# Tracing the first batch's attention without its order behind the latest exponential and maximum

## The chip, the cores and the metric

The kernel runs on one core of a Trainium2 chip. The metric is the device time of one execution in microseconds (us); of the kernel before there are three runs, and their median counts.

Five engines work side by side, each through its own queue of instructions: TensorE (PE, matmuls, with weight loads PEld), VectorE (DVE), ScalarE (ACT), GpSimd (POOL) and SyncE (SP, which here issues nearly all DMAs). Data lies in SBUF; matmuls write to PSUM, which has eight banks per core.

## The reference: what is computed

Attention with a threshold, then a token-mixing block with a channel MLP, then a gated MLP with a convolution over tokens. Cut to what matters (4 batches, 8 heads, 576 tokens, head size 64):

```python
scores = scale * np.matmul(q, k.transpose(0, 1, 3, 2))
thresh = np.max(scores, axis=-1, keepdims=True) - tau
scores = np.where(scores >= thresh, scores, -1e9)
attn = np.exp(scores - np.max(scores, axis=-1, keepdims=True))
attn = attn / (np.sum(attn, axis=-1, keepdims=True) + 1e-09)
x = np.matmul(attn, v)                       # heads side by side: [4, 576, 512]
h = np.maximum(x^T @ w_tok1, 0) @ w_tok2     # token mixing, 576 -> 256 -> 576
u = x + h^T
h2 = np.maximum(u @ w_ch1, 0) @ w_ch2        # channels, 512 -> 1536 -> 512
y = u + h2
g = np.maximum(y @ w_in, 0)                  # 512 -> 1024
out = (g * sigmoid(conv3(g, conv_w))) @ w_out
```

## The kernel before, in words

**Precision and weights.** Most matmuls run on pairs of 16-bit tiles, a high part and the rest; the scores of the first two batches are float32. The weights come as 64-bit numbers and are turned into such pairs once, in pieces of up to 512 columns. Each piece is loaded by SP into one of three stage buffers (`st`, L118), unpacked on ACT (L155, L156), DVE (L157, L159) and sometimes POOL (L153, L143), then split (ACT L144, POOL L145). A stage buffer is free for the next load when L159 has read it.

**Attention.** A batch has four pairs of heads. A pair is worked in nine *slots* of 128 rows of queries (slot 4 of a pair holds 64 rows of either head), so a batch has 36 slots, numbered here through the batch from 0. A slot goes through these steps:

- scores (PE, L308): four matmuls of 128x288 into a pair of PSUM banks; three such pairs take turns in the first batch, so slot i+3 needs mask i to be done
- maximum (DVE, L324, tile `nm`), limit (ACT, L334, `thr`), exponential (ACT, L336), mask (DVE, L343: exponential times "score at least the limit")
- half (ACT, L348: the 16-bit high part), rest (POOL, L352), then a transposing DMA from SP (L357), "transpose i" below
- the product with V (PE, L367 and L370), five slots later

In the first batch the exponential, the halves and the transposed tile of a slot lie in `act_t`, in four sets that take turns: exponential i+4 waits for rest i, half i+4 for transpose i to land, transpose i+4 for product i. After slots 4 and 8 of a pair the products are normalised (DVE L383, L384, L387, L390) and split (ACT L395, POOL L396) into `x`. When both are there, the pair's token mixing follows (`tok`: PE L407 and L422, L427, ACT L412, L429, DVE L413, L430) and gives that pair's part of `u`. The next pair's Q, K and V are loaded by SP (L236, L240, L268) into the tiles of the pair before the last, scaled (ACT L244, POOL L272) and split (ACT L273, POOL L274).

**Dense stages.** `dense(b)` runs the channel MLP and the gated MLP of batch b on PE (L547, L565, L598, L621), and the attention of batch b+1 is traced between its steps. The first of them, L547, needs all four parts of `u`.

**What sets the order.** The program is traced step by step and then put in order by a list scheduler, which gives each engine, in time of its own estimate, the earliest traced instruction whose inputs are ready. The order is fixed when the kernel is built; on the chip an engine takes its instructions in that order. `attention(b)` is a generator with four steps per slot i: exponential work of slot i; mask and half of slot i-1; product of slot i-5, rest and transpose of slot i-1 and scores of slots up to i+2; then the work of `prep` and `tok`. `exps` stores its maximum and its exponential in `crit`. `steps` (L438) wraps the generator and traces each step inside `tc.issue_after` of these two: every ACT instruction of the step gets an edge that keeps it behind the latest exponential traced so far, every DVE instruction one that keeps it behind the latest maximum. These are orders within one queue and cost no semaphore. Only the first batch's attention is wrapped so; the weight steps are traced outside of it.

Of the kernel before, what the change touches and what calls it, by code (L numbers as in the profile page):

```python
# [19 lines left out]
def kernel(ctx: ExitStack, tc: tile.TileContext, q, k, v, tau,  # L20
# [8 lines left out]
    B, NPR, _, S = q.shape  # L29
# [150 lines left out]
    def wstep(n):  # L180

        for _ in range(n):
            while wq and len(wrun) < 3:
                wnext()
            if wrun:
                next(wrun.pop(0))
            if wq:
                wnext()
        if n and not wrun and CB not in free:
            free.append(CB)  # L190
# [106 lines left out]
    def where(i):  # L297
        return i // PER, i // NSL % NP, i % NSL
# [22 lines left out]
    def exps(i):  # L321
        c = chk[i]
        nm = sm.tile([P, 1], F32, tag="nm", name="nm")
        crit["max"] = V.tensor_reduce(out=nm, in_=c["s3"], axis=AX.XY, op=ALU.max, negate=True)  # L324
        kind = 0 if i < NB32 * PER else 1
        bias, sc = nm, 1.0
        if kind:
            bias, sc = sm.tile([P, 1], F32, tag="bias", name="bias"), ESC
            A.activation(out=bias, in_=nm, func=AF.Copy, scale=sc)
        thr = sm.tile([P, 1], F32, tag="thr", name="thr")  # L330
        if kind:
            G.tensor_scalar(out=thr, in0=nm, scalar1=-1.0, scalar2=mtaus[:, 1:2], op0=ALU.mult, op1=ALU.add)  # L332
        else:
            A.activation(out=thr, in_=nm, func=AF.Identity, scale=-1.0, bias=mtaus[:, 0:1])  # L334
        e = half(i, 0).bitcast(F32) if i < PER else qk2.tile([P, S], F32, tag="x", name="e", bufs=15)
        crit["exp"] = A.activation(out=e.rearrange("p (a b) -> p a b", a=2), in_=c["s3"], func=AF.Exp, bias=bias,  # L336
                                   scale=sc)
        c.update(thr=thr, e=e)

    def mask(i):  # L340
        c = chk[i]
        e3 = c["e"].rearrange("p (a b) -> p a b", a=2)
        crit["mask"] = V.scalar_tensor_tensor(out=e3, in0=c["s3"], scalar=c["thr"], in1=e3, op0=ALU.is_ge, op1=ALU.mult)  # L343

    def ph(i):
        c = chk[i]
        c["ph"] = half(i, 1) if i < PER else qk2.tile([P, 2 * S], F16, tag="x", name="ph", bufs=15)
        A.activation(out=c["ph"][:, 0:S], in_=c["e"], func=AF.Copy)  # L348

    def rest(i):  # L350
        c = chk[i]
        G.tensor_tensor(out=c["ph"][:, S:], in0=c["e"], in1=c["ph"][:, 0:S], op=ALU.subtract)  # L352
        if i < PER:
            c["pt"] = half(i, 2).rearrange("p (a b) -> p a b", b=P)
        else:
            c["pt"] = qk2.tile([P, NSL, P], F16, tag="x", name="pt", bufs=15)
        turn[i] = nc.sync.dma_start_transpose(out=c["pt"], in_=c["ph"])  # L357
# [80 lines left out]
    def steps(gen, names):  # L438

        while True:  # L440
            with ExitStack() as held:
                for x in names:
                    if x in crit:
                        held.enter_context(tc.issue_after(crit[x].ins))
                try:
                    next(gen)
                except StopIteration:
                    return
            yield

    def attention(b):

        todo, lag = {}, LAGS[b]

        def start(i, gen, gaps):
            for g in gaps:
                todo.setdefault(i, []).append(gen)
                i += g

        c0, c1 = b * PER, (b + 1) * PER  # L460
        for i in range(c0, c1, NSL):
            bb, p, _ = where(i + NSL)
            if bb < B:
                start(i - 1, prep(bb, p), (1, 2, 2, 1, 1, 1))
            start(i + NSL - 1 + lag + 2, tok(b, where(i)[1]), (2, 1, 1))
        if b == 0:
            for _ in prep(0, 0):
                pass
        i = c0 - 1
        while i < c1 + lag or todo:  # L470
            if c0 <= i < c1:
                exps(i)
            yield
            if c0 <= i - 1 < c1:
                mask(i - 1)
                ph(i - 1)
                if i == PER:
                    free.append(5)
            yield
            if c0 <= i - lag < c1:  # L480
                pv(i - lag)
            if c0 <= i - 1 < c1:
                rest(i - 1)
            for j in range(i + 1, i + (3 if i + 2 < PER else 2)):
                if j < c1 and j not in done:
                    scores(j)
                    done.add(j)
            yield
            for g in todo.pop(i, ()):
                next(g, None)  # L490
            yield
            i += 1
# [159 lines left out]
    W0 = [0, 4, 8, 12, 16, 20, 24, 130]  # L652
    HW, HQ = 32, 35
    behind["qk"] = HQ
    for n, _ in enumerate(steps(attention(0), ("exp", "max"))):
        if n == 13:
            behind["w"] = HW
        wstep(W0.count(n))
    na, nq = n + 1, 2 * NF + 6 * NC + 2 * NG + 4 * (NS + 1)
    for b in range(B):  # L660
        att = attention(b + 1) if b + 1 < B else iter(())
        n = 0
# [65 lines left out]
```

## Time and profile before

| | |
|---|---|
| three runs | 793.1, 795.9, 797.14 us; median 795.9 us |
| the profiled execution | 798.93 us; its span 797.1 us |
| PE busy | 742.8 us, 93% of the span |
| DVE busy | 495.5 us, 62% |
| ACT busy | 471.0 us, 59% |
| POOL busy | 421.8 us, 53% |
| DMA, largest queue (from SP) | 55.0% of 16 engines' time |
| granted TensorE clock, mean | 0.981 of full |

How to read it: PE is busy most of the time, but not evenly. The first 126 us hold the first attention and its handover and have most of the low clock; after 300 us PE is almost never idle. Times inside the span are counted from its start. "Idle before" an instruction is the time in which its engine did nothing ahead of it, with the instruction or DMA that ended that wait.

### The profile page before, as it was taken

To read this page: it belongs to the slowest core of one execution; us is meant where nothing else is said; L and a number is where in the kernel's file an instruction comes from. 1 tells how busy PE (TensorE), PEld (TensorE's weight loads), DVE (VectorE), ACT (ScalarE), POOL (GpSimd) and SP (SyncE) were. 2 spreads that over 40 slices of the span, in tenths; PEclk is the share of its full clock that TensorE was granted. 3 is DMA by queue.
4 is the path that set the end of the run, shared out by engine and by line. 5 is a ranking of instruction groups with operands and counts; after the bars stand their busy time and mean duration, and the time that the engine had idled before them with its cause. 6 is when DMAs were issued, how large, how long until landed. Compare 5 with 4: busy or idle time off the path is not lost. (4 is left out here: it accounts for less than half of the span.)

```text
span 797.1 us, 18473 instructions
## 1 busy us (share of the span) xinstructions
PE 742.8 (93%) x7388; PEld 562.1 (71%) x7388; DVE 495.5 (62%) x837; ACT 471.0 (59%) x998; POOL 421.8 (53%) x471
## 2 busy tenths in 40 slices
PE   5579979898998889999999999999999999999998
PEld 3457657676776675678878875788887856887764
DVE  5568877786767683367677892566876960322370
ACT  6768876775766674466566862566565751220371
POOL 5977788877687572155555771265664840000040
PEclk9889989999999999999999999999999999999999
DMA  9989998888789640368676531667664401000001
GB/s 280 195 186 173 166 240 198 187 226 192 200 219 198 106 76 28 93 135 164 135 164 131 117 54 40 139 134 156 143 133 80 76 18 58 1 1 1 2 1 60
DMA packets 195047, 97.84 MB, mean 123 GB/s; under 512 B 174096, under 2 KB 176656, under 8 KB 194960
## 3 DMA queue, kind: packets, MB, share of 16 engines
q1 hardware_dynamic: 194640, 96.39, 55.0%
q8 instruction: 58, 0.95, 0.5%
q10 hardware_dynamic: 320, 0.26, 0.1%
q14 instruction: 29, 0.24, 0.1%
HBM read 42.36 MB, written 4.72 MB: 59 GB/s over the span
## 5 line engine op out<-in xcount | busy, mean ns | idle before, releaser
L352 POOL TENSOR_TENSOR ph<-e,ph 128x576 f16<-128x576 f32 x108 | 141.2, 1308 | 98.0 <-ACT ph L348 93.0
L565 PE MATMUL ps<-act_t,wc_h 128*128 128x256 f16 (+1 forms) x768 | 148.8, 286 | 0.0
L324 DVE TENSOR_REDUCE nm<-ps 128x1 f32<-128x576 f32 x144 | 108.3, 753 | 54.2 <-PE ps L312 27.0
L308 PE MATMUL ps<-kt,qt 128*128 128x288 f32 (+1 forms) x320 | 95.1, 458 | 27.5 <-DVE act_t L343 12.1
L588 POOL TENSOR_TENSOR act_t<-ct,act_t 128x576 f16<-128x576 f32 x32 | 46.6, 1455 | 138.8 <-ACT act_t L587 135.9
L547 PE MATMUL ps<-u_h,wc_h 128*128 128x256 f16 (+1 forms) x384 | 110.0, 287 | 2.0 <-DVE act_t L522 2.0
L547 PE MATMUL ps<-u_h,wc_l 128*128 128x256 f16 (+1 forms) x384 | 109.9, 287 | 0.0
L565 PE MATMUL ps<-act_t,wc_l 128*128 128x256 f16 (+1 forms) x384 | 109.7, 286 | 0.0
L547 PE MATMUL ps<-u_l,wc_h 128*128 128x256 f16 (+1 forms) x384 | 109.4, 287 | 0.0
L343 DVE SCALAR_TENSOR_TENSOR e<-ps,thr,e 128x576 f32<-128x576 f32 x108 | 87.7, 812 | 22.3 <-ACT e L336 9.8
L547 PEld LDWEIGHTS <-wc_h 128*128 128x128 f16 x768 | 75.4, 98 | 20.3 <-issue 1.3
L565 PEld LDWEIGHTS <-wc_h 128*128 128x128 f16 x768 | 75.0, 98 | 18.9 <-issue 0.5
L308 PEld LDWEIGHTS ps<-kt,qt 128*128 128x128 f32 (+1 forms) x320 | 54.1, 197 | 46.2 <-DVE act_t L343 16.5
L367 PE MATMUL ps<-vh,pt 128*128 128x65 f16 (+1 forms) x1080 | 72.1, 195 | 7.4 <-DMA pt<-ph 7.2
L621 PE MATMUL ps<-wo_h,act_t 128*128 128x512 f16 x256 | 76.3, 379 | 1.8 <-DVE u_l L430 1.3
L583 DVE SCALAR_TENSOR_TENSOR ct<-h,cw,ct 128x576 f32<-128x576 f32 x64 | 68.3, 1068 | 15.2 <-ACT ct L581 14.6
L598 PE MATMUL ps<-u_h,wi_h 128*128 128x256 f16 (+1 forms) x256 | 73.0, 286 | 4.3 <-DVE u_l L430 3.2
L367 PEld LDWEIGHTS <-pt 128*128 128x128 f16 (+1 forms) x1080 | 62.7, 101 | 19.3 <-DMA pt<-ph 10.7
L348 ACT ACTIVATE ph<-e 128x576 f16<-128x576 f32 x108 | 73.0, 676 | 2.1 <-DVE e L343 2.1
L598 PE MATMUL ps<-u_h,wi_l 128*128 128x256 f16 (+1 forms) x256 | 73.0, 286 | 0.0
L598 PE MATMUL ps<-u_l,wi_h 128*128 128x256 f16 (+1 forms) x256 | 73.0, 286 | 0.0
L621 PEld LDWEIGHTS <-act_t 128*128 128x128 f16 x384 | 36.7, 98 | 44.0 <-issue 2.1
(113 smaller groups left out, 1621.3 us busy)
## 6 DMA issues: line engine op xcount, KB each, us to landing
st<-in_moe_w_ch_dram SPq DMA_DIRECT2D x24, 512.0 KB, 4.2
ld<-in_v_dram SPq DMA_DIRECT2D x32, 288.0 KB, 3.4
kt<-ks SPq DMA_DIRECT2D x32, 144.0 KB, 2.7
st<-in_moe_w_in_dram SPq DMA_DIRECT2D x8, 512.0 KB, 4.2
st<-in_moe_w_out_dram SPq DMA_DIRECT2D x8, 512.0 KB, 5.2
out_dram<-ot SPq DMA_DIRECT2D x16, 256.0 KB, 2.0
qt<-in_q_dram SPq DMA_DIRECT2D x8, 288.0 KB, 3.9
kt<-in_k_dram SPq DMA_DIRECT2D x16, 144.0 KB, 3.8
```

The costliest lines, as they stand in the source:

```text
L308: T.matmul(s3[o:o + m, a], f32(st["qt"])[:, q0:q0 + m], f32(st["kt"][hh])[:, a * hn:(a + 1) * hn], start=True, stop=True)
L324: crit["max"] = V.tensor_reduce(out=nm, in_=c["s3"], axis=AX.XY, op=ALU.max, negate=True)
L343: crit["mask"] = V.scalar_tensor_tensor(out=e3, in0=c["s3"], scalar=c["thr"], in1=e3, op0=ALU.is_ge, op1=ALU.mult)
L348: A.activation(out=c["ph"][:, 0:S], in_=c["e"], func=AF.Copy)
L352: G.tensor_tensor(out=c["ph"][:, S:], in0=c["e"], in1=c["ph"][:, 0:S], op=ALU.subtract)
L367: T.matmul(dst[o:o + m], pt[:, j, o:o + m], vh[:, hh, j, 0:D + 1], start=(j == 0), stop=(j == NSL - 1))
L547: T.matmul(t, wc1[wx][:, f, c], u[c][ux][:, sl], start=(c == 0 and i == 0), stop=(c == NC - 1 and i == 2))
L565: T.matmul(t, wc2[wx][:, c, f], r_t(f, rx)[:, sl], start=(by_dve(c) and f == 0 and i == 0), stop=(f == NF - 1 and i == 2))
L583: V.scalar_tensor_tensor(out=ct, in0=ht[:, kk:kk + S], scalar=cw[:, kk, f:f + 1], in1=ct, op0=ALU.mult, op1=ALU.add)
L588: G.tensor_tensor(out=g_t(f, 1), in0=ct, in1=g_t(f, 0), op=ALU.subtract)
L598: T.matmul(t, wi[wx][:, f, c], u[c][ux][:, s0:s0 + n], start=(c == 0 and i == 0), stop=(c == NC - 1 and i == 2))
L621: T.matmul(t, g_t(f, gx)[:, j * P:(j + 1) * P], wo[wx][:, f], **lim)
```

## The change

The wrapper around the first batch's attention goes. `steps` and `crit` stay in the file and no longer do anything.

```diff
-    for n, _ in enumerate(steps(attention(0), ("exp", "max"))):
+    for n, _ in enumerate(attention(0)):
```

The scheduler makes another order of the same work, on all engines, up to a place near 285 us of the trace before; behind it the rows of both orders agree on each engine. Most instructions are moved by a few rows. The places that the prediction speaks of:

On DVE, the maxima of slots 10, 11 and 12 (`nm_490`, `nm_515`, `nm_545`), the masks of slots 9, 10 and 11 (`thr_440`, `thr_492`, `thr_517`), the first pair's first normalisation (`rc_473`, `x32_352`) and two weight steps (`st_225`). Before:

```order
L324 TENSOR_REDUCE nm_490<-ps_166 128x1
L324 TENSOR_REDUCE nm_515<-ps_166 128x1
L157 SCALAR_TENSOR_TENSOR ps_166<-st_225,ps_166 128x288
L383 TENSOR_SCALAR rc_473<-ps_166 128x5
L343 SCALAR_TENSOR_TENSOR act_t_165<-ps_166,thr_440,act_t_165 128x576
L384 RECIPROCAL rc_473<-rc_473 128x5
L387 TENSOR_TENSOR x32_352<-ps_166,rc_473 128x4x64
L390 SCALAR_TENSOR_TENSOR x32_352<-ps_166,rc_473,blk_97 128x128
L343 SCALAR_TENSOR_TENSOR act_t_165<-ps_166,thr_492,act_t_165 128x576
L159 SCALAR_TENSOR_TENSOR wf_224<-st_225,ps_166 128x288
L324 TENSOR_REDUCE nm_545<-ps_166 128x1
L343 SCALAR_TENSOR_TENSOR act_t_165<-ps_166,thr_517,act_t_165 128x576
```

And after the change:

```order
L324 TENSOR_REDUCE nm_490<-ps_166 128x1
L343 SCALAR_TENSOR_TENSOR act_t_165<-ps_166,thr_440,act_t_165 128x576
L324 TENSOR_REDUCE nm_515<-ps_166 128x1
L157 SCALAR_TENSOR_TENSOR ps_166<-st_225,ps_166 128x288
L383 TENSOR_SCALAR rc_473<-ps_166 128x5
L384 RECIPROCAL rc_473<-rc_473 128x5
L324 TENSOR_REDUCE nm_545<-ps_166 128x1
L387 TENSOR_TENSOR x32_352<-ps_166,rc_473 128x4x64
L390 SCALAR_TENSOR_TENSOR x32_352<-ps_166,rc_473,blk_97 128x128
L159 SCALAR_TENSOR_TENSOR wf_224<-st_225,ps_166 128x288
L343 SCALAR_TENSOR_TENSOR act_t_165<-ps_166,thr_492,act_t_165 128x576
L343 SCALAR_TENSOR_TENSOR act_t_165<-ps_166,thr_517,act_t_165 128x576
```

Mask 9 has moved ahead of maximum 11 and the normalisation; mask 10 and L159 have moved behind maximum 12.

On SP, from the load of a weight piece that stands ahead of transposes 8 and 9 (`st_291`) on; `kt1_0_161`, `qt1_160` and `kt1_1_162` are the fourth pair's K and Q. Before, the rows of transposes are 8 and 9, 10 and 11, 12 and 13, 14 to 17:

```order
L118 DMA st_291<-in_moe_w_ch1_dram 128x1024
L357 DMA_TRANSPOSE act_t_165<-act_t_165 128x9x128 x2
L240 DMA kt1_0_161<-in_k_dram 64x576
L118 DMA st_311<-in_moe_w_ch1_dram 128x1024
L357 DMA_TRANSPOSE act_t_165<-act_t_165 128x9x128 x2
L118 DMA st_334<-in_moe_w_ch1_dram 128x1024
L357 DMA_TRANSPOSE act_t_165<-act_t_165 128x9x128 x2
L236 DMA qt1_160<-in_q_dram 128x576
L240 DMA kt1_1_162<-in_k_dram 64x576
L357 DMA_TRANSPOSE act_t_165<-act_t_165 128x9x128 x4
```

After the change they are 8, 9, 10 and 11, 12, 13, 14 to 18:

```order
L118 DMA st_291<-in_moe_w_ch1_dram 128x1024
L357 DMA_TRANSPOSE act_t_165<-act_t_165 128x9x128
L240 DMA kt1_0_161<-in_k_dram 64x576
L357 DMA_TRANSPOSE act_t_165<-act_t_165 128x9x128
L118 DMA st_311<-in_moe_w_ch1_dram 128x1024
L357 DMA_TRANSPOSE act_t_165<-act_t_165 128x9x128 x2
L118 DMA st_334<-in_moe_w_ch1_dram 128x1024
L357 DMA_TRANSPOSE act_t_165<-act_t_165 128x9x128
L236 DMA qt1_160<-in_q_dram 128x576
L357 DMA_TRANSPOSE act_t_165<-act_t_165 128x9x128
L240 DMA kt1_1_162<-in_k_dram 64x576
L357 DMA_TRANSPOSE act_t_165<-act_t_165 128x9x128 x5
```

Transpose 9 has moved behind the first K load and transpose 13 behind the Q load.

On ACT, from the limit of slot 34 (`nm_1367`) to the exponential of slot 36 (`nm_1643`), which is the first of the next batch. The rows of L348 are halves 33, 34 and 35. Before:

```order
L334 ACTIVATE thr_1369<-nm_1367,mtaus_104 128x1
L336 ACTIVATE act_t_165<-ps_166,nm_1367 128x576
L395 ACTIVATE xh_959<-x32_958 128x4x64
L144 ACTIVATE wc1_h_115<-wf_290 128x512
L348 ACTIVATE act_t_165<-act_t_165 128x576
L334 ACTIVATE thr_1392<-nm_1390,mtaus_104 128x1
L336 ACTIVATE act_t_165<-ps_166,nm_1390 128x576
L348 ACTIVATE act_t_165<-act_t_165 128x576 x2
L156 ACTIVATE ps_166<-st_311 128x512
L334 ACTIVATE thr_1645<-nm_1643,mtaus_104 128x1
L336 ACTIVATE e_1647<-ps_166,nm_1643 128x576
```

After the change, halves 33 and 34 alone:

```order
L334 ACTIVATE thr_1369<-nm_1367,mtaus_104 128x1
L336 ACTIVATE act_t_165<-ps_166,nm_1367 128x576
L348 ACTIVATE act_t_165<-act_t_165 128x576
L334 ACTIVATE thr_1392<-nm_1390,mtaus_104 128x1
L336 ACTIVATE act_t_165<-ps_166,nm_1390 128x576
L348 ACTIVATE act_t_165<-act_t_165 128x576
L334 ACTIVATE thr_1645<-nm_1643,mtaus_104 128x1
L144 ACTIVATE wc1_h_115<-wf_290 128x512
L336 ACTIVATE e_1647<-ps_166,nm_1643 128x576
```

Half 35 and the weight step L156 have moved behind the exponential of slot 36, and a weight step L144 stands just ahead of it. On DVE that slot's mask has moved behind the fourth pair's first L383; on POOL the fourth pair's last L396 has moved ahead of the three weight steps that stood before it.

## Rows read from the trace of the kernel before

**Rows 1.** Stages: window, length, busy us per engine, granted clock, DMA share, GB/s.

```profile
20.00:55.00 35.00, 21.59 (x203) 14.97 (x202) 22.44 (x41) 25.72 (x59) 28.47 (x32) 0.84 0.88 181
55.00:97.00 42.00, 39.99 (x504) 30.74 (x505) 33.18 (x60) 35.75 (x77) 32.42 (x33) 0.96 0.96 186
97.00:126.00 29.00, 23.68 (x285) 19.08 (x282) 21.51 (x39) 19.93 (x44) 25.54 (x30) 0.88 1.01 211
126.00:300.00 174.00, 157.47 (x1540) 120.84 (x1539) 129.59 (x213) 120.92 (x255) 129.09 (x137) 0.98 0.78 177
300.00:797.00 497.00, 489.43 (x4839) 369.33 (x4837) 277.55 (x453) 254.80 (x541) 195.25 (x222) 1.00 0.38 83
```

**Rows 2.** PE's waits (total us, times, longest): 20 to 55, 55 to 97, 97 to 126.

```profile
PE ps L308 <- DVE act_t L343: 6.8, 5, 2.9
PE ps L367 <- DMA act_t<-act_t: 6.6, 4, 3.0
...
PE ps L308 <- DVE act_t L343: 1.9, 3, 0.8
...
PE ps L308 <- DVE e L343: 3.1, 2, 2.5
PE ps L367 <- DMA pt<-ph: 2.2, 1, 2.2
```

**Rows 3.** Timeline of DVE (start, length, row): mask 9, mask 10, L159, maximum 12.

```profile
40.02 0.81 DVE L343 SCALAR_TENSOR_TENSOR act_t<-ps,thr,act_t 128x576 f32<-128x576 f32 x1
...
41.55 0.81 DVE L343 SCALAR_TENSOR_TENSOR act_t<-ps,thr,act_t 128x576 f32<-128x576 f32 x1
42.28 0.45 DVE L159 SCALAR_TENSOR_TENSOR wf<-st,ps 128x288 int32<-128x288 int32 x1
43.21 0.76 DVE L324 TENSOR_REDUCE nm<-ps 128x1 f32<-128x576 f32 x1 [0.48 <-PE ps L308]
```

**Rows 4.** Timeline of PE: scores 12, product 8, product 10, scores behind mask 36.

```profile
40.88 2.29 PE L308 MATMUL ps<-kt,qt 128*128 128x288 f32 x4 [0.98 <-DVE act_t L343]
...
47.82 0.20 PE L367 MATMUL ps<-vh,act_t 128*128 128x65 f16 x1 [0.50 <-DMA act_t<-act_t]
...
54.91 0.24 PE L367 MATMUL ps<-vh,act_t 128*128 128x65 f16 x1 [3.02 <-DMA act_t<-act_t]
...
104.42 1.95 PE L308 MATMUL ps<-kt,qt 128*128 128x288 f32 x6 [2.50 <-DVE e L343]
```

**Rows 5.** Timeline of SP's DMA queue: weight load and transposes 8 to 17.

```profile
42.79 0.33 SPq L118 DMA_DIRECT2D st<-in_moe_w_ch_dram  x1
43.29 3.46 SPq L357 DMA_TRANSPOSE act_t<-act_t  x2
...
54.51 3.55 SPq L357 DMA_TRANSPOSE act_t<-act_t  x2
58.58 0.34 SPq L236 DMA_DIRECT2D qt<-in_q_dram  x1
...
59.57 7.49 SPq L357 DMA_TRANSPOSE act_t<-act_t  x4
```

**Rows 6.** Timeline of ACT: half 35, then the exponential of slot 36.

```profile
100.99 0.68 ACT L348 ACTIVATE act_t<-act_t 128x576 f16<-128x576 f32 x1 [2.22 <-DMA act_t<-act_t]
...
102.32 0.71 ACT L336 ACTIVATE e<-ps,nm 128x576 f32<-128x576 f32 x1
```

**Rows 7.** Timeline of POOL: a rest, the first of three weight steps, the split.

```profile
112.48 1.28 POOL L352 TENSOR_TENSOR ph<-e,ph 128x576 f16<-128x576 f32 x1
113.72 1.15 POOL L145 TENSOR_TENSOR wc_l<-wf,wc_h 128x512 f16<-128x512 f32 x1
...
116.57 0.67 POOL L396 TENSOR_TENSOR xl<-x,xh 128x256 f16<-128x256 f32 x1
```

**Rows 8.** DMA issues (count, median us to landing); exponentials' window (busy, count, clock, DMA).

```profile
act_t<-act_t SPq DMA_TRANSPOSE x36, 3.8
...
55.00:97.00 42.00, 13.83 (x19) 0.96 0.96 186
```

## The prediction

> **What bounds the kernel now.** I read the stages first, then what TensorE (PE) waits for in them, and only then single rows. PE is the engine that ends the kernel: from 300 us to the end it is busy 489.43 of 497 us [rows 1], and there the two orders agree on every engine, so that part stays. What the change can give back or cost is PE's idling before. The first batch's attention and its handover to the first dense stage lie between 20 and 126 us: PE idles there for 13.4 us (20 to 55), 2.0 us (55 to 97) and 5.3 us (97 to 126); from 126 to 300 us it idles 16.5 us.
>
> The waits [rows 2] say for whom. From 20 to 55 us PE waits 6.8 us for masks on DVE (L343; a mask frees the PSUM pair that later scores go into) and 6.6 us for transposing DMAs. From 55 to 97 us it waits 1.9 us for masks, from 97 to 126 us 3.1 us for masks and 2.2 us for a transpose. An order on ACT and DVE reaches the masks directly, 11.8 us in all; it reaches the transposes only through what feeds them on POOL and what stands ahead of them on SP.
>
> **The change part by part.** No instruction is added or removed; the edges from all ACT and DVE work of the first attention to its latest exponential and maximum go. The scheduler may then put a mask ahead of the next maximum, a half (L348) ahead of the next exponential, and a normalisation or a V conversion anywhere. The order shows that it does, and that POOL, SP and PE follow. I walk the new order with the durations of the old rows, stage by stage; up to slot 5 almost nothing moves. The sums are differences against the profiled execution (798.93 us, 3.0 us above the median of 795.9), and are then taken off the median.
>
> A, 20 to 55 us (slots 6 to 16). Gain: mask 9 no longer stands behind maximum 11 and the start of the normalisation. It ran at 40.02 us [rows 3], and slot 12's scores waited 0.98 us for it [rows 4]; that wait goes. Loss: mask 10 now stands behind maximum 12, the normalisation's products and the weight step L159. Slot 12's scores then start near 39.9 and, at 2.29 us [rows 4], end near 42.2. Maximum 12 (0.76), the products with their reciprocal (0.72, from the end of mask 9 at 40.83 to mask 10 at 41.55), L159 (0.45) and mask 10 (0.81) follow [rows 3]: mask 10 ends near 45.0, not 42.4, and slot 13's scores wait for it, half a microsecond later than before. L159 itself ends near 44.1, not 42.73. A weight load on SP waits for that step (it was issued at 42.79) and transpose 8 stands behind the load (43.29) [rows 5]. It goes out 1.4 us late; the product on PE that had waited for it until 47.82 [rows 4] starts near 49.2, and slots 15 and 16 come about 1 us late. Then everything meets the product that waits 3.02 us for transpose 10 [rows 4]. That transpose is issued behind a weight load whose own L159 ends, by the same walk, within 0.1 us of before. So A is +0.1: the 3.02 us cover what went before them. Without that cover A would be +1.1; if instead the 0.98 us came through whole and the cover reached only the delays, -1.0.
>
> B, 55 to 97 us (slots 17 to 34). Exponential 16 and mask 16 now precede half 14 and maximum 17, and slot 17's scores go ahead of the token matmuls: about 1 us early each. But PE is already busy for 39.99 of 42 us and the DMA engines for 0.96 of the time [rows 1], so a head start has little room to grow. Against it stand transposes 9 and 13, which now queue on SP behind the fourth pair's K and Q loads. These wait until PE has read the old tiles: the Q load was issued at 58.58 us [rows 5], after slot 17's scores. With those scores 1 us earlier, transpose 13 goes out near 57.9; before it went out near 56.3 (54.51 for transposes 12 and 13, plus half of their 3.55). That is 1.6 us late. What spares it: a half, its rest and a transpose's landing take 0.68, 1.28 and 3.8 us [rows 6 to 8], and the same buffers come round after four slots of 42 / 19 = 2.21 us [rows 8], so 8.84 - 5.76 = 3.1 us are free per round. Products stand in order on PE, though, and one that waits holds all scores behind it. I take +1.0, nearer to the 1.6 than to 0. Its ends: -1.9, all mask waits gone, and +5.2, two full delays of 2.6 (58.58 + 0.34 - 56.3).
>
> The Trainium skill ("DMA: Bandwidth & Descriptors", Latency and other measured facts) gives 261 GB/s for a DMA transpose; for 294,912 bytes that makes 1.13 us, an estimate from that page. Here four in a row take 7.49 us of SP [rows 5], 1.87 us each. By the page the DMA engines would have room to catch up and B's upper end would shrink to near 0, and the sum to -1.9; the measured row decides.
>
> C, the handover (97 to 110 us). Half 35 waited 2.22 us for transpose 31, until 100.99 us, and the next batch's first exponential stood behind it, at 102.32 [rows 6]; its mask released scores that had waited 2.50 us, until 104.42 [rows 4]. Now that exponential stands ahead of half 35 and can start near 100.0. But its mask now stands behind the normalisation's first step (L383), which waits for slot 31's product and so for the same transpose: 101.0, then the product and two small rows (1.1, an estimate from the 0.72 of the three small rows above and about half as much again for the product), then 0.81 for the mask: 102.9 in place of 104.4. C is -1.5. Ends: 0, if the transpose comes later and takes the whole gain, and -3.1, all mask waits of the stage [rows 2].
>
> D, the tail of the fourth pair. On POOL the last split of its x (L396) stood behind three weight steps, from 113.76 (112.48 + 1.28) to 116.57 us [rows 7]: 2.8 us. All three, an L145 of 1.15 us first, now come after it. But all token matmuls of that pair now stand behind a product that waits 2.2 us for a transpose [rows 2], and that transpose gains only one weight load on SP (0.33 [rows 5]). I take -0.5, nearer to the 0.33, between 0 and -2.2.
>
> E, 126 to 300 us. The other weights and the second batch's attention are reshuffled too. PE idles 16.5 us there [rows 1], and nothing in the order says which way that goes: 0, with 2 us either way, about one such wait.
>
> The sum is 0.1 + 1.0 - 1.5 - 0.5 + 0 = -0.9 us: 798.0 against the profiled execution, **795.0 us** against the median.
>
> On the clock: the granted clock is 0.84 of full from 20 to 55 us and 0.96 after it [rows 1], so both levels occur; four score matmuls took 2.29 us in the first stretch, six took 1.95 later [rows 4], 0.57 and 0.33 each. The Trainium skill ("TensorE: Matmul & The Clock Gate", What's actually happening) says that TensorE runs at 1.2 GHz after idling and at 2.4 GHz when kept busy. By it a wait that goes gives back more than its length, up to 1 us per set of four scores, and C would be -2.5. The sum leaves that out, since the waits of 3.02 and 2.22 us ahead of these scores stay.
>
> **The rivals.** First, slower: transposes blocked on SP. Loads that wait for PE now stand ahead of transposes whose input is ready (the fourth pair's K and Q ahead of transposes 9, 13 and 14, the next batch's K ahead of 24). For it: the DMA engines are busy 0.96 of the stage, so a lost place is not made up. Against it: 3.1 us are free per round, and it decides only from there. If transpose 13 and one later one are 2.6 us late on top of that, B is +5.2, the 1.1 of A comes uncovered, and C and D shrink to -1 together: +5.3, or 801.2.
>
> Second, faster: the edges mostly made engines wait. All mask waits from 55 to 126 us (1.9 + 3.1) and the tail's 2.2 us go: -7.2, or 788.7. For it: half 35, which held back a ready exponential. Against it: PE and DMA are nearly full from 55 to 97 us.
>
> Third, the change does nothing for the time: what moves lands in idle time, since each stage ends on the same transposes (10, 31, 35). That is 795.9.
>
> **How the numbers follow.** Half a per cent, 4.0 us, is about what a measurement of this kernel can tell from no change (the three runs lie 4.0 us apart). The forecast gets 0.38, the third case 0.16, the slower rival 0.29, the faster one 0.17. Spread about their centres they make 0.18 faster, 0.51 within, 0.31 slower. The range goes from 789 (just above the faster rival's centre) to 802.5 (the slower one with part of E's 2 us).
>
> **What would show it.** A is right if slot 12's scores wait for no mask, transpose 8 is issued after 44 us, and the product for transpose 10 still starts near 55 us. B is right if PE stays busy for over 38 of the 42 us and the Q load comes just ahead of transpose 13. C is right if slot 36's exponential starts by 100.5 us and PE's 2.5 us wait falls to about 1. D is right if that L396 comes by 115 us and the token matmuls still start after a wait for a transpose. The prediction is wrong if the first dense matmul (L547, near 124.8 us) moves by over 4 us, or if idling in E changes by more than 2 us; the latter would be reshuffling that this reading cannot place.

## The result, and the profile after

The changed kernel took 787.35 us (median of four runs, 784.88 to 790.27) beside 796.52 us for the kernel before: a ratio of 0.9886 with an interval of 0.9847 to 0.9925. Two later sets of runs gave 0.9934 (0.9907 to 0.996; 790.53 beside 795.88 us) and 0.9927 (0.9906 to 0.9947; 792.22 beside 798.3 us). So it is faster by 0.7 to 1.1 per cent, 5 to 9 us, where 0.9 us was forecast. The time of the first set lies below the range's 789, those of the later two inside the range.

The stages after (window, length, busy us of PE, PEld, DVE, ACT, POOL, granted clock, DMA share, GB/s), to be laid beside [rows 1], and the page's line of busy times:

```profile
20.00:55.00 35.00, 22.81 (x246) 15.86 (x246) 23.36 (x43) 28.02 (x62) 31.93 (x36) 0.95 0.97 211
55.00:97.00 42.00, 39.77 (x534) 31.60 (x533) 35.89 (x67) 38.38 (x83) 34.58 (x34) 1.00 1.03 186
97.00:126.00 29.00, 24.07 (x276) 18.22 (x274) 22.49 (x40) 21.10 (x46) 24.24 (x29) 1.00 0.98 241
126.00:300.00 174.00, 159.09 (x1585) 121.83 (x1585) 129.21 (x214) 121.85 (x251) 130.41 (x136) 1.00 0.72 166
```

```profile
PE 731.0 (93%) x7388; PEld 554.2 (71%) x7388; DVE 493.8 (63%) x837; ACT 471.3 (60%) x998; POOL 423.0 (54%) x471
```

The same 7388 matmuls keep PE busy for 731.0 us instead of 742.8. Of the 14.0 us between the two profiled spans (797.1 and 783.1), 11.8 are shorter matmuls and 2.2 are less idling. The granted clock goes with it: 0.95 instead of 0.84 from 20 to 55 us, and 1.00 instead of 0.96, 0.88 and 0.98 in the stages behind. But that profile is of the fastest run of the changed kernel (784.88 us) and has its highest clock, 0.997; its other runs have 0.984 to 0.994. Two more profiles of the same kernel (e1 and e15 below) have PE busy for 736.7 and 736.9 us, so of the 10.3 and 6.6 us that they are shorter than the kernel before, 6.1 and 5.9 are shorter matmuls. Of the stretch from 20 to 300 us the clock was at the lower of its two levels (granted 0.5 of full) for 27.8 us before, and for 3.4, 17.1 and 17.1 us in the three profiles after. The size of 11.8 us is luck of that one execution.

The places that the prediction named, after: PE (products 8 and 10), SP (transposes 8 and 9, the load and transposes 10 and 11, the Q load and transpose 13), ACT (exponential 36, then half 35), and PE's waits from 97 to 126 us.

```profile
45.88 0.20 PE L367 MATMUL ps<-vh,act_t 128*128 128x65 f16 x1 [1.62 <-DMA act_t<-act_t]
50.46 0.20 PE L367 MATMUL ps<-vh,act_t 128*128 128x65 f16 x1 [1.07 <-DMA act_t<-act_t]
```

```profile
41.27 1.31 SPq L357 DMA_TRANSPOSE act_t<-act_t  x1
...
43.56 1.32 SPq L357 DMA_TRANSPOSE act_t<-act_t  x1
45.05 0.46 SPq L118 DMA_DIRECT2D st<-in_moe_w_ch_dram  x1
45.62 3.97 SPq L357 DMA_TRANSPOSE act_t<-act_t  x2
...
52.84 0.57 SPq L236 DMA_DIRECT2D qt<-in_q_dram  x1
53.54 1.28 SPq L357 DMA_TRANSPOSE act_t<-act_t  x1
```

```profile
92.75 0.72 ACT L336 ACTIVATE e<-ps,nm 128x576 f32<-128x576 f32 x1
93.37 0.67 ACT L348 ACTIVATE act_t<-act_t 128x576 f16<-128x576 f32 x1
```

```profile
PE ps L367 <- DMA pt<-ph: 2.7, 3, 1.7
PE ps L422 <- DVE u_l L430: 0.7, 1, 0.7
PE ps L407 <- POOL xl L396: 0.5, 1, 0.5
PE ps L367 <- DMA act_t<-act_t: 0.3, 1, 0.3
PE ps L308 <- DVE e L343: 0.3, 1, 0.3
```

Product 10 starts at 50.46 us, not 54.91 [rows 4], and the wait of 3.02 us is down to 1.07. The first dense matmul (L547) moves by 10.5 us, over twice the 4 that the prediction named as its refutation. The lead grows in two steps, up to slot 16 (5.0 and 4.7 us) and up to exponential 36 (9.5 and 8.1); behind that the two executions of the changed kernel part. Starts in us (exponentials by slot, first matmul of L547, of L621):

| | 8 | 12 | 16 | 35 | 36 | L547 | L621 |
|---|---|---|---|---|---|---|---|
| before | 31.3 | 44.6 | 55.5 | 97.5 | 102.3 | 124.8 | 298.3 |
| after | 32.8 | 42.2 | 50.5 | 89.9 | 92.8 | 114.3 | 283.8 |
| after, third set (e15) | 32.7 | 42.3 | 50.8 | 91.4 | 94.2 | 119.1 | 291.7 |

### The profile page after: what moved, and what is told of

The parts are those of the page before. It is cut to its first block, busy times and chain, and to the rows that moved or that the text cites. A ratio compares the mean times of both kernels' runs of the same rounds, so it can differ in the third digit from the quotient of the medians.

```text
span 783.1 us, 18470 instructions
## 1 busy us (share of the span) xinstructions
PE 731.0 (93%) x7388; PEld 554.2 (71%) x7388; DVE 493.8 (63%) x837; ACT 471.3 (60%) x998; POOL 423.0 (54%) x471
## 5 line engine op out<-in xcount | busy, mean ns | idle before, releaser
L547 PE MATMUL ps<-u_h,wc_h 128*128 128x256 f16 (+1 forms) x384 | 109.7, 286 | 0.8 <-DVE act_t L522 0.8
L547 PE MATMUL ps<-u_h,wc_l 128*128 128x256 f16 (+1 forms) x384 | 109.6, 286 | 0.0
L547 PE MATMUL ps<-u_l,wc_h 128*128 128x256 f16 (+1 forms) x384 | 109.2, 286 | 0.0
L308 PE MATMUL ps<-kt,qt 128*128 128x288 f32 (+1 forms) x320 | 87.8, 433 | 18.6 <-DVE act_t L343 9.0
L547 PEld LDWEIGHTS <-wc_h 128*128 128x128 f16 x768 | 75.1, 98 | 19.9 <-issue 1.3
L583 DVE SCALAR_TENSOR_TENSOR ct<-h,cw,ct 128x576 f32<-128x576 f32 x64 | 68.4, 1069 | 14.8 <-ACT ct L581 14.3
L621 PE MATMUL ps<-wo_h,act_t 128*128 128x512 f16 x256 | 76.3, 379 | 1.5 <-DVE u_l L430 0.9
L308 PEld LDWEIGHTS ps<-kt,qt 128*128 128x128 f32 (+1 forms) x320 | 50.5, 185 | 33.8 <-DVE act_t L343 12.7
L348 ACT ACTIVATE ph<-e 128x576 f16<-128x576 f32 x108 | 73.0, 676 | 2.1 <-DVE e L343 2.1
L621 PEld LDWEIGHTS <-act_t 128*128 128x128 f16 x384 | 36.7, 98 | 43.6 <-issue 1.7
```

Source lines behind the costliest of these rows:

```text
L308: T.matmul(s3[o:o + m, a], f32(st["qt"])[:, q0:q0 + m], f32(st["kt"][hh])[:, a * hn:(a + 1) * hn], start=True, stop=True)
L547: T.matmul(t, wc1[wx][:, f, c], u[c][ux][:, sl], start=(c == 0 and i == 0), stop=(c == NC - 1 and i == 2))
L583: V.scalar_tensor_tensor(out=ct, in0=ht[:, kk:kk + S], scalar=cw[:, kk, f:f + 1], in1=ct, op0=ALU.mult, op1=ALU.add)
L621: T.matmul(t, g_t(f, gx)[:, j * P:(j + 1) * P], wo[wx][:, f], **lim)
```

## The experiments

Ratios are to the kernel before, run beside each; "slot 16" is the start of its exponential in the profiled execution.

**Which part of the order.** In each, `steps` holds only some of the traced steps, or only one engine; four steps belong to a slot. The lines are cut to what differs.

```diff
 e1   after, unaltered
-e2, e3:  steps(attention(0), ("exp", "max"))
+e2:      steps(attention(0), ("exp",))             # ACT held, DVE free
+e3:      steps(attention(0), ("max",))             # DVE held, ACT free
-e4, e5, e8:      for x in names:
+e4, e5:  for x in names if lo <= (n := n + 1) < hi else ():
+e8:      for x in names if not lo <= (n := n + 1) < hi else ():
+e4:      lo, hi = 0, 72       # held up to slot 16, free behind
+e5:      lo, hi = 72, 1000    # free up to slot 16, held behind
+e8:      lo, hi = 32, 72      # free for slots 7 to 16 alone
```

> The changed kernel again, unaltered, for the granted clock of each of its runs and of the runs of the kernel before on the same chip. In the two profiles TensorE is busy 742.8 us before and 731.0 us after for the same 7388 matmuls, and idle 54.3 and 52.1 us. Theory of the clock: the gain is mostly matmuls that no longer run at the low level behind long waits; then the runs of the kernel before show a mean granted clock near 0.98, those of the changed one near 0.99, a ratio near 0.989 again, and within each kernel the runs with the higher clock are the shorter ones. Theory of the waits alone: the clocks of the two do not differ on average (both 0.98 to 0.99), and the ratio is still near 0.989, since the waits themselves became 9 us shorter.

> Only ACT work is kept behind the latest exponential; DVE is free. If the gain comes from DVE (masks ahead of the next maximum, so that scores start sooner): the ratio stays near 0.989 to 0.992. If it comes from ACT (halves that no longer hold back or wait for exponentials): 0.996 to 1.000.

> DVE keeps its order behind the latest maximum, ACT is free. Transpose 5 stands behind the weight load st_266, as before. If the effects of DVE's and ACT's orders add, this is what the unaltered change gains beyond freeing DVE alone: 5.4 - 3.8 = 1.5 us, so 794.3. Theory T: transpose 3 lands over 5 us after its issue and exponential 12 is not sooner than 44 us; 794.5 to 798. Theory D (DVE's order is what counts): 795 to 797, as the kernel before.

> The old order is kept for the steps up to slot 16 (the stretch of 20 to 55 us, where the clock fell in the kernel before after waits of 1.6, 2.6 and 3.0 us) and dropped behind it. If the gain is made up to slot 16: at most a third of it is left, ratio 0.996 to 1.000 (793 to 796.5 us). If it is made from slot 17 on, at the handover to the dense stage above all (clock falls behind waits of 2.5 and 2.2 us at 104 and 116 us): ratio 0.989 to 0.992 (788 to 790 us).

> The reverse: no order up to slot 16, the old order from slot 17 on. If the gain is made up to slot 16: ratio 0.989 to 0.992. If it is made from slot 17 on: 0.996 to 1.000. If the two halves add up, this and the reverse together give the whole 9 us.

> The order behind the latest exponential and maximum is dropped for the steps of slots 7 to 16 alone; the slots before and after keep it. Transpose 5 stays behind the weight load st_266. On DVE mask 9 comes ahead of maximum 11, and mask 10 and L159 come behind maximum 12, as walk A of the prediction had it. Theory T (walk A was right for these slots; what it missed is transpose 5): transpose 3 lands over 5 us after its issue, transpose 8 is issued at 43.5 or later, the product that waits for transpose 10 starts near 54.5; time 794.5 to 798. Theory D: transpose 8 by 42.5, exponential 12 by 43.2, exponential 16 by 52.5; time 790.5 to 793.

| | free | ratio | slot 16 |
|---|---|---|---|
| e1 | all | 0.9934 (0.9907 to 0.996) | 50.8 |
| e2 | DVE | 0.9963 (0.9939 to 0.9987) | 52.5 |
| e3 | ACT | 0.9982 (0.9956 to 1.0007) | 50.9 |
| e4 | behind slot 16 | 1.0047 (1.0022 to 1.0071) | 55.1 |
| e5 | up to slot 16 | 0.9942 (0.9917 to 0.9966) | 51.6 |
| e8 | slots 7 to 16 | 0.9969 (0.9946 to 0.9993) | 50.4 |

What is gained is gained early, though not always kept: e5 and e8 have slot 16 four to five us sooner and keep 0.3 to 0.6 per cent, while e3 has it 4.6 us sooner and its ratio can't be told from 1. Freeing only the later steps (e4) makes the kernel slower. In e4 one token matmul waits for a split on POOL between 126 and 300 us, a wait that neither the kernel before nor the changed one has there (waits of PE: total, times, longest):

```profile
PE ps L367 <- DMA pt<-ph: 6.1, 6, 1.8
PE ps L407 <- POOL xl L396: 3.2, 1, 3.2
```

Few of the ranges were met: e4 and e5 lie outside both of theirs, and e2, in the range named for ACT, is still faster than the kernel before. In e8 transposes 3 and 8 went as theory D had it (4.0 us to landing, issue at 39.7 us), but its time of 794.33 us lies between the ranges of D and T.

**A theory that fell.** In the kernel before, transpose 3 landed 5.5 us after its issue, in the changed one after 3.9. The view of one tile in a stretch (SP's instruction, its length in ns; who waited; issue to landing), before and after:

```profile
L357 SPq DMA_TRANSPOSE act_t<-act_t x1: 1866/1866/1866, 29.9 to 29.9; - x1
...
DMA to landing us min/median/max: 5.5/5.5/5.5
```

```profile
L357 SPq DMA_TRANSPOSE act_t<-act_t x1: 1887/1887/1887, 29.6 to 29.6; - x1
...
DMA to landing us min/median/max: 3.9/3.9/3.9
```

On SP the weight load st_266 stands between transposes 4 and 5 before, and behind transpose 5 after. That was my first suspicion.

```diff
+e7 (before):  tc.add_manual_dep(loads[7].ins, turn[5].ins.name, ...)   # st_266 behind transpose 5
+e6 (after):   with tc.issue_after(loads[7].ins) if i == 5 else nullcontext(): turn[i] = ...
```

> The kernel before, all orders kept, but the weight load st_266 now stands on SP behind transpose 5 instead of ahead of it, as in the changed kernel (the only other difference: one weight step L155 on ACT comes after slot 10's exponential). Theory T (the load, following two transposes, makes the first of them land late, and the slots after it hang on that): transpose 3 lands 3.9 to 4.0 us after its issue instead of 5.5; PE's 2.62 us wait shrinks to under 0.7; the product of slot 4 starts 1.0 to 1.6 us sooner; transpose 8 goes out near 41.5 (43.29 before), exponential 12 near 42.8 (44.6), exponential 16 near 52.5 (55.5); time 791 to 793.5. Theory D (the gain is DVE's order, masks ahead of maxima): whatever transpose 3 does, exponential 12 stays within 0.6 us of 44.6 and the time at 795 to 797.

> The changed kernel with one thing put back: transpose 5 stands behind the weight load st_266 on SP, as before the change. Up to about slot 18 every other engine keeps the changed order; later rows are reshuffled. Theory T: transpose 3 lands 5.3 to 5.6 us after its issue, so slot 4's product and slot 12's scores come 1.3 to 2 us later than in the changed kernel, transpose 8 is issued near 43 to 44 (41.3 there), exponential 12 near 44 (42.3 there), exponential 16 after 53; time 793 to 797. Theory D: exponential 12 by 42.9, exponential 16 by 51.5, time within 1.5 us of the changed kernel's 790.5.

With the load moved away (e7) transpose 3 still took 5.2 us, and the ratio was 1.0006 (0.9977 to 1.0034). With the load put back (e6) it took 3.9. So the load's place doesn't make it late. But e6 also came out at 1.0026 (1.0005 to 1.0048) although its slot 16 starts at 51.3: the scheduler had put the rows behind slot 18 into another order, and from slot 16 to 36 it took 48.5 us where e1 took 42.4. A small edge early was thus followed by later rows that took longer by more than the whole gain.

**Packets on another queue.** What did move with transpose 3 was a packet on the queue q8. The page of before counts 58 of them (packets, MB, share):

```profile
q8 instruction: 58, 0.95, 0.5%
```

One is in the stretch from 33.0 to 33.1 us; the second fence is the DMA line of 34 to 36 us (busy share in slices of 0.05 us, tenths):

```profile
q8 instruction: 1, 0.02, 77.9%
```

```profile
DMA  0000001001000000000004999999999999939854
```

For about 1.1 us the DMA engines do nearly nothing, with transposes 3 and 4 not yet landed. Another packet came at 52.8 us, and transpose 10, whose product had the wait of 3.02 us, took 5.9 us. After the change the packets came at 33.4 and 51.0 us, when transpose 3 was all but down (33.5) and transpose 10 had landed (50.4); transposes 4 and 11, then in flight, took 5.1 and 6.1 us (4.3 and 5.5 before). The other traces bear this out for transpose 3. In the 13 without idle pairs, these two among them, whatever their order, it took 5.2 to 5.6 us in the four where the packet came between 32.7 and 33.3 us, and 3.8 to 4.0 us in the nine where it came at 33.4 or later. One of these nine is e11 below, which has the order of the kernel before up to there. If q8 brings PE's instructions (0.95 MB over 14,776 matmuls and weight loads is 64 bytes each), then instructions that do nothing, ahead of the first scores, must move the packets against the work. The pairs of weight load and matmul write a PSUM column that nobody reads; the order of all other rows is the same on every engine.

```diff
+    for _ in range(32):     # e9 (before), e13 (after); 16: e14 (before), e10 (after); 48: e18, e17
+        T.matmul(ps[:, 7, 400:401], ident, ident[:, 0:1], start=True, stop=True)
     W0 = [0, 4, 8, 12, 16, 20, 24, 130]
```

> The kernel before with 32 idle pairs of weight load and matmul (128x1) on PE ahead of its first scores; all other orders are the same on every engine. Theory F: the queue q8, which moves 58 packets of 16 KB in the kernel before, brings PE's instructions, and for about 1.1 us after such a packet the transposes in flight stand still; in the kernel before the packets of 33.0 and 52.8 us hit transposes 3 and 10. With 64 more instructions ahead, the packets come two products sooner in PE's stream: near 25 to 27 us, where no transpose but 2 is in flight, and near 47 to 49 us. Then transpose 3 lands 3.9 to 4.3 us after its issue (5.5 before), transpose 10 under 5 us (5.9), exponential 12 comes 0.6 to 1.5 us sooner and exponential 16 1.5 to 2.5 us sooner; time 1 to 3 us below the kernel before. Rival theory O (ACT's held order makes transpose 3 late): it lands 5.2 to 5.6 us after its issue, and the time is that of the kernel before.

> The changed kernel with 16 such idle pairs on PE ahead of its first scores, all other orders the same. Theory F: the packets that came at 33.4 and 51.0 us, just when transposes 3 and 10 had landed, come one product and one set of scores sooner, near 30 and 48 to 49 us, and hit both: transpose 3 lands 4.8 us or more after its issue (3.9 in the changed kernel), transpose 10 5.5 us or more (4.8); exponential 16 comes 0.8 to 2 us later; time 1 to 2.5 us above the changed kernel's (790.5 to 787). Rival theory O: 3.9 to 4.1 and 4.8 us, time unchanged.

> The changed kernel with 32 idle pairs of weight load and matmul (128x1) on PE ahead of its first scores, as e9 has them in the kernel before; all other orders the same. Theory S (the new order saves by itself, the packets' places come on top): q8's packets come near 26 and 44 us, transpose 3 lands 3.8 to 4.3 us after its issue, exponential 16 at 50 to 51.8 us, time 3 to 6 us below e9's 0.9966 of the kernel before, so a ratio of 0.989 to 0.993. Theory L (what the change gained is mostly that its packets miss transposes 3 and 10): a ratio of 0.995 to 0.999, as e9.

> The kernel before with 16 idle pairs: packets near 29 to 30 and 49 to 50 us, so transposes 3 and 10 are still hit. If the packets' places are what e9 gained by: transpose 3 4.6 us or more and transpose 10 5.5 us or more after their issues, exponential 16 at 54.5 to 56, ratio 0.998 to 1.002. If the idle pairs gain by themselves (PE warmer at the start): ratio 0.995 to 0.998 as in e9.

> The changed kernel, unaltered, beside e13 and e14. Both theories: ratio 0.988 to 0.994 to the kernel before, exponential 16 at 50.5 to 51, transpose 3 landing 3.9 to 4.1 and transpose 10 4.8 us after their issues. A ratio above 0.996 would say that the gain isn't steady from one set of runs to the next.

> The changed kernel with 48 idle pairs on PE ahead of its first scores, all other orders the same. q8's packets should come three products sooner than without pairs: near 22 to 24 us and near 41 to 44 us, so that transpose 1, and transpose 8 or 9, are hit and 3 and 10 are spared. Theory L (over places of the packets the two orders are worth the same): within 0.5 per cent of the kernel before with the same 48 pairs. Theory S (the changed order is better except where a packet hits transpose 8): at least 0.4 per cent faster than that kernel if transpose 8 lands under 5.5 us after its issue.

> The kernel before with the same 48 idle pairs. Packets near 22 to 24 and 40 to 42 us; transpose 3 lands 3.9 to 4.2 and transpose 10 under 5 us after its issue, exponential 16 at 53 to 54; ratio to the kernel before 0.993 to 0.999, as with 16 and 32 pairs, where both transposes were spared at least in part.

Packets (q8, start of the half microsecond in which each came, of the kernel before its time) and issue to landing of transposes 3, 8 and 10 (us); the two rows with 16 pairs come from different sets of runs, as do those with 32:

| pairs ahead | order | packets | 3 | 8 | 10 | slot 16 | ratio |
|---|---|---|---|---|---|---|---|
| 0 | before | 33.0, 52.8 | 5.5 | 4.5 | 5.9 | 55.5 | 1 |
| 0 | after (e15) | 33.5, 51.0 | 3.8 | 4.8 | 5.0 | 50.8 | 0.9927 (0.9906 to 0.9947) |
| 16 | before (e14) | 29.5, 51.0 | 4.4 | 4.4 | 4.9 | 52.9 | 0.9948 (0.9929 to 0.9967) |
| 16 | after (e10) | 29.5, 50.0 | 4.7 | 4.7 | 6.7 | 51.1 | 0.9936 (0.991 to 0.9962) |
| 32 | before (e9) | 26.0, 42.0 | 3.9 | 5.4 | 4.9 | 53.7 | 0.9966 (0.9943 to 0.9989) |
| 32 | after (e13) | 25.5, 45.5 | 4.2 | 7.2 | 4.8 | 53.4 | 1.0033 (1.0015 to 1.0051) |
| 48 | before (e18) | 23.5, 41.0 | 3.8 | 4.9 | 4.9 | 52.5 | 1.0023 (0.9993 to 1.0052) |
| 48 | after (e17) | 23.5, 42.5 | 4.1 | 5.2 | 5.0 | 52.8 | 0.9978 (0.9949 to 1.0007) |

The packets moved, and the late landings went with them: transpose 3 lost its delay, transpose 10 lost it or got it, and with 32 pairs in the changed order a packet at 45.8 us caught transpose 8. Its view and the row of product 8, which waited 1.62 us in the changed kernel:

```profile
L357 SPq DMA_TRANSPOSE act_t<-act_t x1: 1282/1282/1282, 41.1 to 41.1; - x1
...
  PE ps L367: 4.1, 1
...
DMA to landing us min/median/max: 7.2/7.2/7.2
```

```profile
48.29 0.20 PE L367 MATMUL ps<-vh,act_t 128*128 128x65 f16 x1 [4.07 <-DMA act_t<-act_t]
```

A late landing alone is no sign of a packet, though: in e8 transpose 9, behind a weight load and a K load, took 5.6 us with no packet on q8 from 33.9 to 48.4 us.

The times say more than I had asked for. The same order of the same work spreads from 0.9948 to 1.0023 (before) and from 0.9927 to 1.0033 (after), with nothing changed but idle pairs that take 1.0 us of an idle PE in e13. Against the same number of pairs the changed order stands at -0.7, -0.1, +0.7 and -0.4 per cent. Their mean is -0.16 per cent, 1.2 us, with an uncertainty of about 0.3 per cent from their scatter: not to be told from zero, nor from the 0.9 us forecast. In the profiled executions, one each, the changed order is ahead at L547 with every number of pairs (by 10.5, 5.7, 5.6 and 0.1 us); with 16, 32 and 48 pairs it loses that again, and takes 175.6, 178.2 and 175.2 us from L547 to L621 where the old order takes 167.5, 170.2 and 171.3.

Misses, too: e9's second packet came at 42 us, not 47 to 49; e14 spared transpose 10 and gained as much as e9, which is nearest to the rival that idle pairs gain by themselves; e10 came out no slower than the changed kernel; e13 lies above the ranges of both theories; the two kernels with 48 pairs lie 0.4 per cent apart, which fits theory L and theory S alike; e18 spared both transposes, was ahead at slot 16 (52.5), and yet its ratio lies above 1, which speaks against the idle pairs gaining by themselves. Two packets of 58 don't explain a time. Later packets do have quiet stretches behind them: in all 19 traces from 28 to 126 us, a stretch of 0.7 us or more in which less than 25 GB/s were started on q1, the queue of nearly all DMAs, begins between 0.2 us ahead of a packet and 1.4 us behind it for 87 of 148 packets on q8, and for 5 per cent of the places that lie 2 us or more from any packet of q8 or q14. What they cost in time is not shown, and the idle pairs also start PE earlier.

**The handover alone.** Step C by itself, in the kernel before (e11), and with e8's window (e12):

```diff
+        if i == 36: tc.add_manual_dep(turn["half", 35].ins, crit["exp"].ins.name, ...)   # half 35 behind exponential 36
```

> The kernel before with one edge more: half 35 behind the exponential of slot 36 (step C of the prediction by itself). Up to there all orders are those of the kernel before; the rows behind are put anew by the scheduler. By the prediction: exponential 36 starts at 100 to 100.7 us (102.3), the scores that waited 2.5 us wait about 1, and from there on all is 1.5 us sooner with E at 0 plus or minus 2: 794 to 796.5 where the kernel before has 796 to 797.5. Rival (E was mis-sized: each new order of the rows behind is worth 4 to 8 us either way): exponential 36 is as much sooner, and yet the time lies more than 3 us off, below 793 or above 799.

> The two pieces together: the order behind the latest exponential and maximum dropped for the steps of slots 7 to 16 alone, and half 35 behind the exponential of slot 36. If the pieces add: 3.2 us of the first and 1.5 us of the second, 791 to 793.5 where the kernel before has 796 to 797.5. If the order of the rows behind slot 36 decides: anywhere from 787 to 798.

ACT in e11, exponential 36 and then half 35:

```profile
98.27 0.72 ACT L336 ACTIVATE e<-ps,nm 128x576 f32<-128x576 f32 x1
99.32 0.68 ACT L348 ACTIVATE act_t<-act_t 128x576 f16<-128x576 f32 x1 [0.33 <-DMA act_t<-act_t]
```

Exponential 36 starts 2.6 us after exponential 35 (95.7), not 4.9 as before: the 1.5 us that C forecast are there, and more. The time is 1.0022 (1.0001 to 1.0042) all the same (799.41 us; the rival had it above 799), and e12 has 0.9969 (0.9946 to 0.9993), just what e8 has without the edge. From L547 to L621 e11 took 175.6 us and e12 176.0, where the kernel before took 173.5 and e8 169.7. So what the handover wins was given back behind it. That the new order of the rows there did it is argued: with one and the same order this stretch took from 167.5 to 173.5 us in the executions of the kernel before with and without idle pairs, and 169.6, 174.0 and 172.6 us in three of the changed kernel. In e11 all rows up to slot 36 stand as in the kernel before, and there the packet came at 34.6 us, transpose 3 landed after 3.9 us and slot 16 started at 53.8: up to there the profiled execution of the kernel before, with 55.5, had been an unlucky one. Beside e11 the changed kernel's slot 16 is 3.3 us sooner, not 5.0.

## Why the prediction was wrong

**A failed**, and with it the sum. It said +0.1 us; slot 16 came 5.0 us sooner. Its first claim held: slot 12's scores no longer wait for mask 9. Three steps of it didn't. The rows on which this rests are, before, two sets of scores on PE and the L159 ahead of transpose 10 on DVE; and after, three sets of scores, the last of them slot 12's, and that L159:

```profile
28.32 1.24 PE L308 MATMUL ps<-kt,qt 128*128 128x288 f32 x4 [2.91 <-DVE act_t L343]
36.16 2.27 PE L308 MATMUL ps<-kt,qt 128*128 128x288 f32 x4
48.03 0.45 DVE L159 SCALAR_TENSOR_TENSOR wf<-st,ps 128x288 int32<-128x288 int32 x1
```

```profile
28.08 2.29 PE L308 MATMUL ps<-kt,qt 128*128 128x288 f32 x4 [3.22 <-DVE act_t L343]
34.39 1.24 PE L308 MATMUL ps<-kt,qt 128*128 128x288 f32 x4 [0.17 <-DVE act_t L343]
37.72 1.24 PE L308 MATMUL ps<-kt,qt 128*128 128x288 f32 x4
44.53 0.45 DVE L159 SCALAR_TENSOR_TENSOR wf<-st,ps 128x288 int32<-128x288 int32 x1
```

- "Slot 12's scores then start near 39.9": they started at 37.7. The walk kept everything up to product 4 at its old time. But transpose 3 landed 1.8 us sooner, and the scores behind it ran at the full clock (1.24 us for four, where the kernel before took 2.27). So maximum 12 and L159 came sooner, and transpose 8 went out at 41.27 us; the prediction had 44.7, before it was 43.29 [rows 5].
- "Own L159 ends, by the same walk, within 0.1 us of before": the L159 ahead of transpose 10 started at 44.53, not 48.03. Of these 3.5 us the 3 by which maximum 13 already came sooner (42.77 for 45.82) are the larger part; the rest is that L159 now precedes maximum 14 instead of waiting behind it. Transpose 10 went out 3.4 us sooner.
- "Then everything meets the product that waits 3.02 us": that wait was taken as a fixed wall. About 1.1 us of it, an estimate from the length of the quiet stretch, was the packet. In the changed order the packet came after the landing. Idle pairs alone cut the wait in the old order, too, to 0.55 us in e9 and 0.53 in e14; but there product 8 then waited 3.04 and 2.06 us, not 0.50, so a wait went as well as moved.

**The clock was left out of the sum** because "the waits of 3.02 and 2.22 us ahead of these scores stay". They didn't. Between the profiles this was the largest term: 11.8, 6.1 and 5.9 us of 14.0, 10.3 and 6.6 are shorter matmuls, against a sum of -0.9 that had none. The sentence from the Trainium skill ("TensorE: Matmul & The Clock Gate", What's actually happening) had the right direction, and the trace agrees with it in part: in the changed kernel four scores took 2.29 us behind a wait of 3.22 us (from 28.08 us) and 1.24 us behind one of 0.17 (from 34.39), but in the kernel before four took 1.24 us behind one of 2.91 (from 28.32). The length of the last wait alone doesn't tell the level.

How much of the gain the clock is, over many runs, is less sure. In 33 runs of the kernel before, 791.7 to 799.8 us, the mean granted clock went from 0.976 to 0.990 and the time fell by 4.7 us per 0.01 of it (correlation -0.75); in the other four sets of its runs by 2.5 to 3.8 (-0.41 to -0.71). The two kernels' mean clocks differ by 0.004 in e1's set (0.983 and 0.987) and by 0.008 in e15's (0.981 and 0.989). By these sets' own rates (4.7 and 2.9 us) that is about 2 of 5 us and 2 of 6, an estimate, so over many runs the clock need not be the larger part. Nor does it go with the order alone: from 20 to 300 us it was at its lower level for 14.2, 17.8 and 23.9 us in the old order with 16, 32 and 48 idle pairs, and for 23.6, 20.5 and 28.1 us in the changed one.

**B** (+1.0, from -1.9 to +5.2): from exponential 16 to 35 it took 41.9 us before and 39.4 after. With 16, 32 and 48 pairs it is 42.1, 41.3 and 42.6 after against 43.2, 41.8 and 40.8 before. So between -2.5 and +1.8: the size is not settled by the order. The signs named held: PE busy for 39.77 of 42 us, the Q load just ahead of transpose 13 (52.84 and 53.54). Transpose 13 had gone out at 55.9 us before, 0.4 sooner than the prediction took it to. The delay was covered, as the 3.1 us per round said it might be: product 13 waited 0.29 us for its transpose.

**C** was right in mechanism and nearly in size: -1.5 forecast, and 2.0 us less from exponential 35 to 36 (4.9 to 2.8); PE's wait for that mask fell from 2.5 to 0.3 us, further than the 1 us named. Transpose 31, for which half 35 waited, was met by a packet on q8 before (97.2 us) and after (89.4 us) and took 4.8 and 4.9 us, so the packets don't make this difference. e11 shows the step alone.

**D** (-0.5): from exponential 36 to L547 22.5 us before, 21.5 after, 20.6 in e1, but 24.9 in e15. The sign can't be told. The sign named, that L396 comes by 115 us, held (107.53) only since all came sooner: it started 14.3 us behind exponential 36 before and 14.8 after, and PE still waited 0.5 us for it.

**E** (0, 2 us either way) had too narrow a range. The idling from 126 to 300 us fell from 16.5 to 14.9, within the 2 us; but in the orders of e5 and e6 it is 12.1 and 20.5, 4 us either way, and the range should have held that. How much of it is the order is open, since the old order alone, with 16, 32 and 48 idle pairs, has 12.9, 14.4 and 16.8.

**The rivals.** The faster one had about the size (788.7) and not the reason. Its mask waits did go, from 5.0 to 0.3 us, but other waits took their place: PE idled 7.3 us from 55 to 126 us before and 7.2 after. The slower one did not happen: no product waited over 0.5 us for a transpose from 52 to 88 us. A time like its 801.2 came in another kernel, e4, whose longest wait of that stage was for a split on POOL and not for SP.

**What stays open.** The unaltered change is faster in all three sets, that is shown. So is it that late landings of transposes 3, 8 and 10 follow the packets on q8. That its order is better by itself is not shown: with other numbers of idle pairs it gains and loses in turn. What makes the time of one placement differ from another's, packets, clock or later rows, stays open too.

## What to carry to other kernels

A reordering that gains or loses under one per cent should be measured again with a few idle instructions ahead of the bounding engine; if the sign turns, the gain belongs to where things happen to fall and not to the order. When a long wait in a trace serves as cover or wall in a sum, look first whether that instance took longer than its siblings, and why. And price a wait of an often idle PE with the clock behind it, but take that price from several traces: here one kernel had the low clock for 3.4 us in one execution and for 17.1 in two others, from 20 to 300 us.

## What the runs showed of the hardware

The packets of 16 KB on q8 move with PE's instructions: 64 more of them ahead brought the packet from 33.0 to 26.2 us. Behind these packets the DMA engines stood nearly still for about 1.1 us (34.0 to 35.1, 53.6 to 54.7), as they did behind 87 of the 148 counted above, and a transpose in flight landed after up to 7.2 us; of those in the table that no packet met, none took over 5.0. Whether the packets of 8 KB on q14 do the same is open: such a stretch lies behind 20 of the 88 that have no packet of q8 within 1.5 us. In e13, DMA's GB/s from 45 to 49 us in slices of 0.1 us show such a stretch from 46.1 on:

```profile
GB/s 5 10 18 113 274 297 289 451 269 401 46 0 0 0 0 0 0 8 8 8 10 10 10 8 31 300 369 369 49 54 148 225 177 228 205 215 151 289 287 294
```

Why one packet of 16 KB stops all sixteen engines for that long, no run here shows.
